# A second buffer for turned keys, and a planner that counts what transfers bring or free as coming later

## The chip, the cores and the metric

The kernel runs on one core of a Trainium2 chip. The metric is device time in microseconds (us). The engines are PE (TensorE, matrix products), DVE (VectorE), ACT (ScalarE), POOL (GpSimd) and SP (SyncE, which here issues every DMA of the kernel body). Each engine works through a list of instructions in a fixed order and waits on semaphores for what the others bring.

## The reference

Block-sparse attention over 4 batches, 8 heads, 768 tokens and 64 features, whose result goes through a feed-forward net with a rational activation:

```python
mask = np.abs(blk_i - blk_j) <= 1            # blocks of 32 tokens, 24 of them
mask = mask | (blk_i == 0) | (blk_j == 0) | (blk_i == n_blocks - 1) | (blk_j == n_blocks - 1)
for qb in range(n_blocks):
    for kb in sampled_blocks[qb]:            # 3 sampled blocks
        mask[qb * 32:(qb + 1) * 32, kb * 32:(kb + 1) * 32] = True
scores = np.where(mask, q @ k.T / sqrt(64), -1e9)
x = softmax(scores) @ v                      # then 3072 tokens of 512 features
h = x @ w_in                                 # w_in 512 x 2048
P = a[0] + a[1] * h + a[2] * h**2 + a[3] * h**3
Q = 1.0 + abs(b[0]) * abs(h) + abs(b[1]) * h**2
out = (P / (Q + 1e-6)) @ w_out               # w_out 2048 x 512
```

## The kernel before

**The work.** The feed-forward net is cut into 12 chunks of 256 tokens, each of 8 units of 256 hidden features, 96 units in all (`unit(c, u)`). PE multiplies a unit into the hidden layer (L1147 to L1149, three products because numbers are kept as a high and a low f16 part), ACT and DVE form the rational function (`sq`, `ab`, `tt`, `rr`, `gh`, `gl`), and PE multiplies it out into `acc` (L1203 to L1205). Attention feeds it: for each block of 32 queries PE makes scores `sp` (L909), DVE the maxima (L919), ACT the exponentials (L937), PE turns them (`pt`, L978), ACT copies them (`pT`, L151), and PE multiplies by the gathered values `vg` (`av`, L1035). Keys come in per block from a scratch array `ks` in DRAM into one of four buffers (`kall` in three parts, and `xkg`), values from `v` into one of three buffers `vg`. Both are loaded by SP: one key or value block is a group of four to six DMAs, three of them at sampled rows (L881, L1005).

**Keys of a batch.** `prep(b)` reads the keys of batch b twice: once for their largest magnitude (ACT, `scrap<-ld`, L398) and once to split them into f16 parts `hl`, which PE turns (`sp<-ident,hl`, L684) into one of two PSUM buffers `sp`. ACT copies these into `kt` (four copies of 0.7 us to a `kt`, L151), and SP stores `kt` into `ks` (L698). A batch has three `kt`. Before the change there is one `kt` buffer, so the copies for the next `kt` wait until the store has read the last one. The same six load buffers `ld` also carry the values, whose largest magnitudes are found by `scrap<-ld` too, and for batches 2 and 3 the queries. For batch 0 the turned keys stay in SBUF.

**The planner.** The order on each engine is not written out. Every step is an `Op` with an engine, a price in ns, a due time and the buffers that it takes and uses; `issue` picks, again and again, the step that could start first by its own clock, and appends it to its engine. A buffer ring (`Ring`) knows when each buffer is free again. A transfer is priced with 475 to 860 ns on SP per DMA, and by its bytes after that. A step that depends on another gets an earliest start `at`, and a later `sure` by which it is ranked; a step of PE that waits for another engine is ranked 1000 ns later. During the first 80 us of its clock it puts dummy products (L163) where it sees PE idle. When the weights are decoded, `switch` closes the pool `early` and opens `ext` with four more `ld` and one more key buffer.

**The start.** Until the first chunk is ready (unit 0), SP loads keys, queries and values of batch 0 and the first pieces of `w_in` (`wl`, L439); POOL, ACT and DVE decode these from 64-bit numbers and split them (`wi`, L155, L512).

Of the kernel before, what the change touches and what calls it, by code (L numbers as in the profile page):

```python
# [13 lines left out]
F16 = mybir.dt.float16  # L14
# [9 lines left out]
def kernel(  # L24
# [28 lines left out]
    B, H, S, D = q.shape  # L53
    DM, DFF = out.shape[1], w_out.shape[0]
    P = 128
    BLK = 32
# [18 lines left out]
    p1 = ctx.enter_context(tc.tile_pool(name="p1", bufs=1))  # L75
    p2 = ctx.enter_context(tc.tile_pool(name="p2", bufs=2))
    p3 = ctx.enter_context(tc.tile_pool(name="p3", bufs=3))
# [18 lines left out]
    VE, SC, PO, TE, SY = "DVE", "Activation", "Pool", "PE", "SP"  # L96
# [68 lines left out]
    def issue(ahead):  # L165
        def work_of(t, price, share):
            for x in (int(t / 3413), int(t / 3413) + 1):
                busy[x] = busy.get(x, 0.0) + share * max(0.0, min(t + price, (x + 1) * 3413) - max(t, x * 3413))

        def tick(t):  # L170
            nonlocal window, warm
            while window < int(t / 3413):
                share = busy.pop(window, 0.0) / 3413
                warm, window = share > (0.45 if warm else 0.85), window + 1

        todo = {e: [] for e in (VE, SC, PO, TE, SY, None)}
        now = dict.fromkeys(todo, 500.0)
        held = 0.0, 0.0
        clock, dma, lanes, quarters = -1.0, 0.0, [0.0] * 8, False
        busy, window, warm = {}, 0, False  # L180
        for n, o in enumerate(plan):
            o.n, o.wait = n, len(o.after) + (o.behind is not None)
            for a in o.after:
                a.next.append(o)
            if o.behind:
                o.behind.next.append(o)
            if not o.wait:
                for e in o.engs:
                    todo[e].append(o)
        left = len(plan)  # L190
        fsh = 0.8
        other = {VE: 500, SC: 534.0, PO: 243.0}
        unit_of = {VE: nc.vector, SC: nc.scalar, PO: nc.gpsimd}
        slack, fend, f00, fgap = 21.0, 80000, 3000, 0
        while left:
            best = None
            for e, l in todo.items():
                for o in l:
                    if o.prio > clock + ahead or not all(s.ring.free for s in o.takes):
                        continue  # L200
                    t = max([now[e], o.at[e]] + [s.ring.free[0][0] for s in o.takes])
                    if e == SY:
                        t = max(t, lanes[0])
                    if e == VE and held[0] <= t < held[1] and o.run.__name__ not in READS_PSUM:
                        t += HELD * (held[1] - t)
                    sure, same = max(t, o.sure[e]), e != TE or o.quarters == quarters
                    key = (max(sure - slack, now[e]) + (0 if e == o.engs[0] else other[e]) + (0 if same else 0), o.prio - (0 if e != TE or not same else 1.0), o.n)
                    if best is None or key < best[0]:
                        best = key, t, o, e
            if best is None:  # L210
                lim = [o for l in todo.values() for o in l]
                raise AssertionError([(o.eng, o.prio, o.run.__qualname__, [len(s.ring.free) for s in o.takes]) for o in lim][:40] + [clock])
            _, t, o, o.eng = best
            e = o.eng
            for x in o.engs:
                todo[x].remove(o)
            for s in o.takes:
                s.buf = s.ring.free.pop(0)[1]
            price = o.alt[e] if o.alt else o.price() if callable(o.price) else o.price
            o.start = t  # L220
            if isinstance(price, list):
                for ns, size in price:
                    t = max(t, lanes.pop(0) if e == SY else t) + ns
                    dma = max(dma, t + 650) + size / 225.0
                    if e == SY:
                        lanes.append(dma + 900)
                end = dma + 900
            elif e == TE:
                f0 = max(now[e], f00)
                while f0 < fend:  # L230
                    tick(f0)
                    f = 213 if warm else 427
                    if f0 + f + fgap > t:
                        break
                    fill()
                    work_of(f0, f, 1.0)
                    f0 += f
                tick(t)
                if now[e] < fend:
                    w = window  # L240
                    x0 = w * 3413
                    for _ in range(2):
                        if not warm or t - x0 < 700 or busy.get(w, 0.0) >= fsh * (t - x0):
                            break
                        fill()
                        work_of(t, 213, 1.0)
                        t += 213
                if not warm:
                    price *= 2 if price > 1100 or price < 500 else 1.8
                if o.quarters != quarters:  # L250
                    t += 93
                    quarters = o.quarters
                work_of(t, price, o.work)
                end = t = t + price
            else:
                end = t = t + price
            now[e] = t
            if e == PO:
                held = o.start, end
            o.end = end  # L260
            o.run(unit_of[e]) if o.alt else o.run()
            if o.unit is not None:
                clock = max(clock, o.unit)
            for s in o.uses:
                s.left -= 1
                s.end = max(s.end, end + (0 if isinstance(price, list) else 200))
                if not s.left:
                    s.ring.free.append((s.end, s.buf))
                    s.ring.free.sort(key=lambda f: f[0])
            for x in o.next:  # L270
                if x.behind is not o:
                    for y in x.engs:
                        lat = MARGIN if isinstance(price, list) else OWN.get(e, 0) if y == e else LAT.get((e, y), 160) + MARGIN
                        x.at[y] = max(x.at[y], end + lat)
                        x.sure[y] = max(x.sure[y], end + lat + (1000 if y == TE and e != TE else 0.0))
                x.wait -= 1
                if not x.wait:
                    for y in x.engs:
                        todo[y].append(x)
            left -= 1  # L280
# [3 lines left out]
    r_gh, r_gl = Ring([None] * 2), Ring([None] * 2)  # L284
    r_ph, r_sp, r_pt, r_acc = Ring([None] * 2), Ring([None] * 2), Ring([None]), Ring([None])
    r_pr, r_st, r_pT, r_av = Ring([None] * 4), Ring([None] * 6), Ring([None] * 2), Ring([None] * 4)
    r_ld, r_hl, r_kt = Ring([p3] * 3), Ring([None] * 2), Ring([None])
    r_ldq, r_hlq, r_qa, r_fc, r_ks = Ring([None]), Ring([None]), Ring([None] * 2), Ring([None] * 2), Ring([None] * 2)
    r_cq, r_scq, r_xn, r_sm = Ring([None] * 4), Ring([None] * 3), Ring([None]), Ring([None] * 2)
    r_wl, r_dw, r_kx, r_sums = Ring([None] * 2), Ring([None] * 3), Ring(range(2)), Ring([None] * 2)  # L290
# [232 lines left out]
    kgs = [kall[:, i * NS:(i + 1) * NS] for i in range(NB // NS)]  # L523
# [113 lines left out]
    s_kt, kts, ext = {}, {}, []  # L637

    def rest(b, w, j, d, o_scale, sc, prio, before):
        first = b == 0  # L640
        t, g = units[j]
# [44 lines left out]
        def evac(e):  # L686
            def run(eng):
                if g == 0 and e == 0:
                    kts[b, t] = kgs[t] if first else p1.tile([P, KB, H, BLK], F16, name="kt")
                dst = kts[b, t][:, :, g * HU:(g + 1) * HU].rearrange("p b h (r s) -> p s h b r", s=2)[:, e]  # L690
                src = d["pt"][:, e].rearrange("p h (b r) -> p h b r", b=KB)
                times(eng, dst, src, 1.0)
            return run
# [7 lines left out]
        sk = s_kall[t] if first else s_kt[b]  # L701
# [612 lines left out]
    for b in range(B):  # L1314
        if b:
            prep(b, when(b))
        for t in range(NT):
            x0 = min(x for x, p in enumerate(parts) if p[0] == b and p[1] // TB == t)
            before = prep_q(b, t, -78.95 if b == t == 0 else part_prio(x0) - (3.23 if x0 >= need[0] else 12.17), before)
            for j in range(t * TB, (t + 1) * TB):  # L1320
                x = next(x for x, p in enumerate(parts) if p[:2] == (b, j))
                attention(b, j, part_prio(x))

    for c, u in order:
        b = c // NCH
# [6 lines left out]
    def switch():  # L1332
        early_cm.__exit__(None, None, None)
        ext.append(ctx.enter_context(tc.tile_pool(name="ext", bufs=1)))
        t = max(o.end for o in decoded + last_near)
        r_ld.free += [(t, ext[0])] * 4
        for j in range(1):
            kgs.append(ext[0].tile([P, NS, H, BLK], F16, name=f"xkg{j}"))
            r_kg.free.append((t, len(kgs) - 1))

    Op(None, 0, switch, decoded + last_near, -1)
    ctx.enter_context(tc.manual_schedule(engines={getattr(mybir.EngineType, n) for n in (TE, SC, VE, PO, SY)}))
    issue(8)
# [29 lines left out]
```

## Time and profile before

| | us |
|---|---|
| median of 3 runs (lowest, highest) | 880.39 (877.9, 882.73) |
| the profiled execution | 884.24 |
| its span on the core | 882.5 |
| PE busy in the span | 814.4 (92%) |
| DVE busy | 729.4 (83%) |
| ACT busy | 668.8 (76%) |
| POOL busy | 115.5 (13%) |

The span is what the trace shows; the execution's time is 1.7 us longer. PE's busy time holds the dummy products of the start, 53.8 us in 201 instructions. The engines' busy times overlap, so a share says little by itself: what counts is when PE stands still, and what it waits for.

### The profile page before, as it was taken

What the parts mean: (1) busy time and instruction counts of PE and PEld (TensorE: products, weight loads), DVE (VectorE), ACT (ScalarE), POOL (GpSimd) and SP (SyncE); (2) the same over time, 40 slices, a digit from 0 to 9 for tenths busy, and PEclk for the clock granted to TensorE, in tenths of its full rate; (3) what the DMA queues carried; (4) which work ended last, traced back from release to release, by engine and by line L of the source; (5) the groups of instructions that cost most, each with busy time, mean ns of one, the idle gap of its engine ahead of it and who ended that gap; (6) DMA issues with size and microseconds to landing.
All of it is one profiled execution on the core that took longest, in us unless ns stands there. A gap on an engine that the chain in (4) does not pass through costs nothing.

```text
span 882.5 us, 27191 instructions
## 1 busy us (share of the span) xinstructions
PE 814.4 (92%) x10339; PEld 648.8 (74%) x10339; DVE 729.4 (83%) x1749; ACT 668.8 (76%) x1445; POOL 115.5 (13%) x119
## 2 busy tenths in 40 slices
PE   8979677777999999999998999969999999999997
PEld 4545565565877788878886888847888888888886
DVE  5667987999997889978895888668788887888996
ACT  6878876996776887898776877948867777776563
POOL 2132631706310000110000000000000000000000
PEclk9999898898999999999999999979999999999999
DMA  7898599785865977889757975787757856560000
GB/s 207 198 175 209 152 195 192 200 217 145 224 160 141 262 205 178 207 235 220 188 144 189 251 204 156 183 222 183 204 148 171 201 141 164 148 160 26 1 25 25
DMA packets 240210, 151.17 MB, mean 171 GB/s; under 512 B 16208, under 2 KB 222928, under 8 KB 240080
## 3 DMA queue, kind: packets, MB, share of 16 engines
q1 hardware_dynamic: 240080, 149.43, 68.5%
q8 instruction: 82, 1.34, 0.7%
q14 instruction: 48, 0.39, 0.2%
HBM read 132.07 MB, written 11.01 MB: 162 GB/s over the span
## 4 chain that ended last, share of the span: by engine, by line
PE 52%; DVE 15%; ACT 13%; DMA 10%; SPq 6%; issue 4%; POOL 0%; ACTq 0%; DVEq 0%; POOLq 0%
PE acc L1203 7%; PE acc L1205 6%; PE acc L1204 6%; PE ph L1147 6%; PE ph L1149 6%; PE ph L1148 6%; PE av L1035 4%; PE pt L978 4%; PE sp L909 3%; DMA vg<-in_v_dram 3%; ACT pr L937 3%; DVE pr L919 2%; PE acc L163 2%; ACT scrap L398 2%; ACT kt L151 2%
## 5 line engine op out<-in xcount | busy, mean ns | idle before, releaser
L1147 PE MATMUL ph<-xh,wi 128*128 128x256 f16 x768 | 213.1, 277 | 7.5 <-DVE tt L1164 7.5
L1148 PE MATMUL ph<-xl,wi 128*128 128x256 f16 x768 | 212.3, 276 | 0.0
L1149 PE MATMUL ph<-xh,wi 128*128 128x256 f16 x768 | 212.1, 276 | 0.0
L1203 PE MATMUL acc<-wo_h,gh 128*128 128x512 f32 x376 | 161.2, 429 | 2.2 <-DVE ld L1263 2.2
L1205 PE MATMUL acc<-wo_h,gl 128*128 128x512 f32 x376 | 150.4, 400 | 0.0
L1204 PE MATMUL acc<-wo_l,gh 128*128 128x512 f32 x376 | 150.3, 400 | 0.0
L1171 DVE SCALAR_TENSOR_TENSOR ab<-sq,absb,ab 128x512 f32<-128x512 f32 x96 | 73.2, 763 | 48.3 <-ACT ab L1168 47.8
L1154 ACT ACTIVATE sq<-ph,fc 128x512 f32<-128x512 f32 x96 | 65.5, 682 | 61.4 <-PE ph L1149 61.3
L937 ACT ACTIVATE pr<-pr,st,cqb 128x256 f32<-128x256 f32 x112 | 66.2, 595 | 41.8 <-DVE st L948 41.8
L1147 PEld LDWEIGHTS <-wi 128*128 128x128 f16 x768 | 76.6, 100 | 24.5 <-issue 13.2
L919 DVE CUSTOM_DVE_ANT_1 pr<-sp,bias 128x256 f32<-128x256 f32 x224 | 84.1, 417 | 10.6 <-PE sp L909 10.6
L1148 PEld LDWEIGHTS <-wi 128*128 128x128 f16 x768 | 76.3, 99 | 15.7 <-issue 6.9
L978 PE MATMUL pt<-ident,pr 128*128 128x128 f32 x448 | 76.0, 292 | 11.6 <-ACT pT L151 7.4
L1203 PEld LDWEIGHTS acc<-wo_h,gh 128*128 128x128 f32 x376 | 72.6, 193 | 18.5 <-issue 2.6
L1182 DVE SCALAR_TENSOR_TENSOR gh<-tt,par,rr 128x512 fp32r<-128x512 f32 x96 | 72.5, 755 | 16.0 <-PE acc L1204 14.2
L1205 PEld LDWEIGHTS acc<-wo_h,gl 128*128 128x128 f32 x376 | 71.8, 191 | 17.4
L1149 PEld LDWEIGHTS <-wi 128*128 128x128 f16 x768 | 76.3, 99 | 9.8
L978 PEld LDWEIGHTS pt<-ident,pr 128*128 128x128 f32 x448 | 66.0, 206 | 22.4 <-ACT pT L151 11.9
L1204 PEld LDWEIGHTS acc<-wo_l,gh 128*128 128x128 f32 x376 | 72.3, 192 | 12.0
L1035 PE MATMUL av<-vg,pT 128*32 128x64 f32 x3584 | 71.4, 224 | 8.0 <-DMA vg<-in_v_dram 5.9
L1035 PEld LDWEIGHTS av<-vg,pT 128*32 128x32 f32 x3584 | 56.5, 111 | 29.7 <-issue 19.2
L1188 DVE SCALAR_TENSOR_TENSOR tt<-tt,par,ab 128x512 f32<-128x512 f32 x96 | 74.8, 779 | 0.9
(164 smaller groups left out, 1670.4 us busy)
## 6 DMA issues: line engine op xcount, KB each, us to landing
vg<-in_v_dram SPq DMA_DIRECT2D x312, 64.0 KB, 3.5
vg<-in_v_dram SPq DMA_DIRECT2D x88, 192.0 KB, 4.4
vg<-in_v_dram SPq DMA_DIRECT2D x24, 512.0 KB, 5.0
kall<-ks SPq DMA_DIRECT2D x52, 192.0 KB, 4.0
kall<-ks SPq DMA_DIRECT2D x156, 64.0 KB, 2.6
ld<-in_k_dram SPq DMA_DIRECT2D x36, 256.0 KB, 4.3
wl<-in_moe_w_in_dram SPq DMA_DIRECT2D x32, 256.0 KB, 4.7
wl<-in_moe_w_out_dram SPq DMA_DIRECT2D x16, 512.0 KB, 4.8
```

What stands on the lines that cost most here:

```text
L919: nc.vector.tensor_tensor_reduce(out=prs[x][:, g].rearrange("p (s r) -> p s r", r=BLK), in0=h["sp"][:, g].rearrange("p (s r) -> p s r", r= ...
L937: nc.scalar.activation(out=prs[x][:, g], in_=prs[x][:, g], func=AF.Exp, scale=Q["first"]["c"], bias=st[:, 6 + g:7 + g], accum_out=total if ...
L978: nc.tensor.transpose(pp[:, jj * P:(jj + 1) * P], cols, ident)
L1035: nc.tensor.matmul(av[rows, g], pT[:, 2 * g + kt, rows] if plain else pT[:, 2 * g + kt, pa_, rows], vf[:, g * HG + h4, kt * D:(kt + 1) * D ...
L1147: nc.tensor.matmul(o, wh, xh[:, :, cc], start=(cc == 0), stop=False)
L1148: nc.tensor.matmul(o, wh, xl[:, :, cc], start=False, stop=False)
L1149: nc.tensor.matmul(o, wl, xh[:, :, cc], start=False, stop=(cc == NCC - 1))
L1171: nc.vector.scalar_tensor_tensor(out=d["ab"], in0=d["sq"], scalar=absb[:, 1:2], in1=d["ab"], op0=ALU.mult, op1=ALU.add)
L1188: nc.vector.scalar_tensor_tensor(out=d["tt"], in0=d["tt"], scalar=par[:, 0:1], in1=d["ab"], op0=ALU.add, op1=ALU.subtract)
L1203: nc.tensor.matmul(acc[:, t], ghs, wo_h[:, f], start=(new and e == 0), stop=False)
L1204: nc.tensor.matmul(acc[:, t], ghs, wo_l[:, f], start=False, stop=False)
L1205: nc.tensor.matmul(acc[:, t], gls, wo_h[:, f], start=False, stop=(last and e == 1))
```

## The change

Four edits. In `issue`, a buffer that a transfer has used counts as free 2000 ns after the transfer's planned end instead of at it, and a step that depends on a step of SP is ranked 2000 ns later. `kt` takes its buffer from a pool that the ring names, and `switch` adds a second one from `ext`, so that from then on (batches 2 and 3) two `kt` are in use.

```diff
             for s in o.uses:
                 s.left -= 1
-                s.end = max(s.end, end + (0 if isinstance(price, list) else 200))
+                s.end = max(s.end, end + (2000 if isinstance(price, list) else 200))
...
-                        x.sure[y] = max(x.sure[y], end + lat + (1000 if y == TE and e != TE else 0.0))
+                        x.sure[y] = max(x.sure[y], end + lat + (1000 if y == TE and e != TE else 0.0) + (2000 if e == SY else 0.0))
...
-    r_ld, r_hl, r_kt = Ring([p3] * 3), Ring([None] * 2), Ring([None])
+    r_ld, r_hl, r_kt = Ring([p3] * 3), Ring([None] * 2), Ring([p1])
...
-                    kts[b, t] = kgs[t] if first else p1.tile([P, KB, H, BLK], F16, name="kt")
+                    kts[b, t] = kgs[t] if first else sk.buf.tile([P, KB, H, BLK], F16, name="kt")
...
         r_ld.free += [(t, ext[0])] * 4
+        r_kt.free += [(t, ext[0])]
```

The two numbers of the planner change the order on every engine from the first microseconds up to about unit 64; behind that, PE's order is the same as before. The work is the same but for two more dummy products (203 for 201) and for steps that may run on either of two engines: POOL gets three fewer conversions, DVE two fewer, ACT five more.

Three places follow. The first is ACT in batch 3, where the keys are copied into `kt` (the numbers tell buffers apart: `ld_10194` is a part of the values, `kt_10354` the second of the three). Before:

```order
L1158 ACTIVATE tt_10257<-ph_10127,par_100,fc_8026 128x512
L151 ACTIVATE pT_10275<-pt_10251 128x512
L1178 ACTIVATE rr_10247<-rr_10247 128x512
L398 ACTIVATE scrap_103,mx_9961<-ld_10194 128x512
L1175 ACTIVATE rr_10318<-ab_10243 128x512
L1178 ACTIVATE rr_10318<-rr_10318 128x512
L151 ACTIVATE kt_10354<-sp_10202 128x4x8x16
L151 ACTIVATE kt_10354<-sp_10261 128x4x8x16
L151 ACTIVATE kt_10354<-sp_10202 128x4x8x16
L151 ACTIVATE kt_10354<-sp_10261 128x4x8x16
```

The same place of ACT now (`kt_10254` is the second `kt`):

```order
L151 ACTIVATE kt_10169<-sp_10184 128x4x8x16
L937 ACTIVATE pr_10049,sm_9925<-pr_10049,st_10048,cqb_6708 128x256 x2
L151 ACTIVATE kt_10254<-sp_10224 128x4x8x16
L1154 ACTIVATE sq_10263<-ph_10151,fc_8043 128x512
L151 ACTIVATE kt_10254<-sp_10224 128x4x8x16
L1168 ACTIVATE ab_10268<-ph_10151,fc_8043 128x512
L1175 ACTIVATE rr_10288<-ab_10108 128x512
L151 ACTIVATE pT_10307<-pt_10270 128x512
L151 ACTIVATE kt_10254<-sp_10279 128x4x8x16
L1178 ACTIVATE rr_10288<-rr_10288 128x512
L151 ACTIVATE kt_10254<-sp_10279 128x4x8x16
```

The second `kt` now begins right behind the first, each `sp` buffer is emptied in turn, and the maximum of a part of the values that stood ahead of the copies has moved behind all twelve of them.

The second place is SP where it asks for the queries of batch 3 (the larger rows around them are one key block ahead and one value block behind). Before:

```order
L881 DMA kall<-ks 128x256
L767 DMA qc<-qa 64x1024
L768 DMA qc<-qa 64x1024
L729 DMA ldq<-in_q_dram 64x4x128 x2
L596 DMA ld<-in_q_dram 128x512 x4
L999 DMA vg_109<-in_v_dram 48x8x128
```

Now, with two value blocks still to come that stood ahead of the query loads before:

```order
L881 DMA kall<-ks 128x256
L596 DMA ld<-in_q_dram 128x512 x3
L999 DMA vg_110<-in_v_dram 48x8x128
L1005 ISA
L1005 DMA vg_110<-in_v_dram 16x8x128
```

The query loads have moved ahead of two value blocks, of an exchange of query halves (L767, L768) and of another load.

The third place is SP in the start, between the first four DMAs of `w_in` (two pieces) and the fourth piece. Before:

```order
L439 DMA wl<-in_moe_w_in_dram 64x1024 x4
...
L768 DMA qc<-qa 64x1024
L596 DMA ld<-in_k_dram 128x512 x3
L439 DMA wl<-in_moe_w_in_dram 64x1024 x2
L999 DMA vg_109<-in_v_dram 48x8x128
...
L439 DMA wl<-in_moe_w_in_dram 64x1024 x2
L999 DMA vg_110<-in_v_dram 48x8x128
```

Now:

```order
L439 DMA wl<-in_moe_w_in_dram 64x1024 x4
L596 DMA ld<-in_k_dram 128x512 x3
...
L439 DMA wl<-in_moe_w_in_dram 64x1024 x2
...
L999 DMA vg_109<-in_v_dram 48x8x128
...
L999 DMA vg_110<-in_v_dram 48x8x128
...
L999 DMA vg_111<-in_v_dram 48x8x128
...
L439 DMA wl<-in_moe_w_in_dram 64x1024 x4
```

The fourth piece stood behind one value block and now stands behind three; the fifth comes with it.

## Rows read from the trace of the kernel before

**Rows 1.** The page: PE's busy share in 40 slices of the span, in tenths.

```profile
PE   8979677777999999999998999969999999999997
```

**Rows 2.** Busy time by stages: length, engines, PE's clock, DMA share, GB/s.

```profile
core 0: us, PE busy (x) PEld busy (x) DVE busy (x) ACT busy (x) POOL busy (x), PEclk, DMA share, GB/s
0.00:72.50 72.50, 62.76 (x790) 34.08 (x791) 44.91 (x155) 53.25 (x138) 19.81 (x29) 0.95 0.87 192
72.50:187.20 114.70, 86.80 (x1326) 66.10 (x1325) 101.91 (x251) 95.18 (x223) 47.74 (x43) 0.90 0.84 193
187.20:257.10 69.90, 61.75 (x783) 48.83 (x781) 69.10 (x168) 53.36 (x113) 28.75 (x24) 0.95 0.69 181
257.10:840.00 582.90, 565.05 (x7221) 469.08 (x7221) 480.00 (x1130) 446.47 (x941) 19.24 (x23) 0.99 0.69 174
```

**Rows 3.** PE's waits: who waited for whom, us in total, times, longest.

```profile
PE sp L684 <- ACT kt L151: 12.9, 3, 7.7
...
PE av L1035 <- DMA vg<-in_v_dram: 5.9, 4, 3.2
PE pt L978 <- ACT pr L937: 4.1, 1, 4.1
```

**Rows 4.** The chain of work that ended last, 563 to 587 us: start, length.

```profile
563.90 0.46 PE sp L684 x8
...
574.33 4.18 DMA ld<-in_v_dram
...
578.53 0.72 ACT scrap L398 x2
...
579.43 3.86 DMA ks<-kt
...
583.32 1.90 ACT kt L151 x3
...
585.26 1.01 PE sp L684 x8
```

**Rows 5.** Busy time around that wait, columns as in rows 2.

```profile
580.00:585.00 5.00, 0.00 (x0) 0.00 (x0) 2.80 (x4) 2.12 (x4) 0.26 (x1) 0.56 0.85 242
585.00:590.00 5.00, 4.74 (x31) 3.15 (x31) 1.53 (x3) 3.17 (x7) 0.69 (x1) 0.50 1.08 238
590.00:595.00 5.00, 5.00 (x40) 4.26 (x39) 4.91 (x14) 2.67 (x7) 0.00 (x0) 0.91 0.92 268
```

**Rows 6.** The tile kt: its copies, waits, and its stores' time to landing.

```profile
L151 ACT ACTIVATE kt<-sp x36: 711/735/787, 154.6 to 597.0; 128x512 f16<-128x512 f16 x36
...
  DMA ks<-kt: 3.2, 2
...
DMA to landing us min/median/max: 3.7/4.5/5.2
```

**Rows 7.** SP at 472 us and before 576 us, instructions in order of time: start, length.

```profile
472.01 2.02 SPq L596 DMA_DIRECT2D ld<-in_q_dram  x4
...
572.81 1.42 SPq L881 DMA_DIRECT2D xkg<-ks  x3
574.33 1.66 SPq L596 DMA_DIRECT2D ld<-in_v_dram  x1
```

**Rows 8.** ACT's wait for queries of batch 3, and busy time after it.

```profile
ACT scrap L398 <- DMA ld<-in_q_dram: 8.4, 1, 8.4
...
478.00:480.00 2.00, 1.96 (x9) 1.38 (x10) 0.25 (x1) 2.00 (x5) 0.00 (x0) 0.56 1.25 184
480.00:485.00 5.00, 5.00 (x31) 3.98 (x30) 4.61 (x9) 5.00 (x13) 0.00 (x0) 0.84 0.90 192
```

**Rows 9.** SP in the start, columns as in rows 7.

```profile
44.29 0.54 SPq L999 DMA_DIRECT2D vg<-in_v_dram  x1
...
50.55 0.38 SPq L999 DMA_DIRECT2D vg<-in_v_dram  x1
```

**Rows 10.** SP's longest wait between 420 and 580 us.

```profile
SPq L876 <- PE av L1035: 1.6, 1, 1.6
```

## The prediction

> **What bounds the kernel now.** I read first the page's slices [rows 1]: after a start with gaps PE is at 9 tenths nearly everywhere from the eleventh slice on, but for an 8 at the twenty-second (463 to 485 us) and a 6 at the twenty-seventh (573 to 596). The table of stages gives the sizes [rows 2]. Up to unit 0 (72.5 us) nothing but dummy products keeps PE busy, and the weights have to come in. From 72.5 to 187.2 us (unit 8) PE lacks 27.9 us while DVE is busy 101.91 of 114.70: DVE, which decodes weights, is the limit. From 187.2 to 257.1 DVE has 69.10 of 69.90, so it is DVE again. From 257.1 to 840 PE has 565.05 of 582.90 at a clock of 0.99: PE is the limit, it lacks 17.9 us, and a wait of PE there moves the end by its length. So I looked for PE's longest waits [rows 3]: `sp` for ACT's copies of turned keys, 12.9 us in 3 waits with a longest of 7.7; the values `vg`, 5.9 in 4; and once 4.1 for the exponentials.
>
> The chain around 580 us shows what the 7.7 are made of [rows 4]. A load of values is issued at 574.33 and has landed at 578.51; behind it ACT finds a maximum, then waits until the store `ks<-kt`, 3.86 us, has ended at 583.3, then copies keys, and PE goes on at 585.26. The clock charges for this once more [rows 5]: in 580 to 585 PE does nothing, and in 585 to 590 its granted clock is 0.50, that is 1.2 in place of 2.4 GHz. Busy time at half clock is worth half: 4.74 × 0.50 = 2.4 us lost, then 5.00 × 0.09 = 0.45, together **2.8**. The Trainium skill ("TensorE: Matmul & The Clock Gate", section Terms) says the same in its formula for the penalty, throttled time times one less the ratio of pulses passed; the trace agrees with it here: eight products of L684 take 1.01 us in the chain's last row at this clock, and took 0.46 in its first [rows 4].
>
> **The change part by part.**
>
> *The second `kt`.* All copies to `kt` are 36 of about 0.735 us, and ACT waits for stores twice, 3.2 us in all [rows 6]. The longer of these, nearly all, is the one in the chain. With a second buffer ACT needn't wait for the store between the first and the second `kt` of batch 3. By itself this is worth at most the 3.86 us of the store in the chain, since the load of values ahead of it in ACT's order still lands at 578.5. The third `kt` now waits for the first store; four copies (2.9 us) lie between and a store takes 4.5 from issue, so without anything between them 1.5 us of wait would be left; the rows of the order show other work of ACT between the copies, which covers it. I take 0.
>
> *The maximum of values behind the copies.* The rank given to what depends on SP moves that step behind all twelve copies. Its load stood behind three key DMAs on SP [rows 7], and ACT stood for it with all its queue: the exponentials, the copies, half of the rational function. Where it now stands, the load has several copies' time (twelve × 0.735 = 8.8 us) more to land, against 4.18 from issue to landing. So the whole PE wait goes, 7.7, and the half clock behind it, 2.8: **−10.5**.
>
> *The queries of batch 3.* ACT waits 8.4 us for them at 467.5 to 475.9 [rows 8]; they are issued at 472.01 [rows 7]. PE waits only the last 4.1 of it [rows 3], so an ACT wait of up to 8.4 − 4.1 = 4.3 is free there. The clock then stands at 0.56 and 0.84: 1.96 × 0.44 + 5.00 × 0.16 = 1.7 lost [rows 8]. On SP the loads have moved ahead of two value blocks, and two of these take 6.3 us of SP in the start (44.29 to 50.55 in [rows 9]), more than the 4.1 that are needed; they have also moved ahead of three other groups. ACT's own step may come earlier too; the 4.3 that are free stand against that. Taken as gone: −4.1 − 1.7 = **−5.8**.
>
> *What is given back.* SP has no slack to do all this: between 420 and 580 us its longest wait is 1.6 us [rows 10], so each load that is moved ahead makes another one later. The two value blocks behind the queries are those, and laid against before's times I find one more such place near 276 us and one near 452 us, with values about 3 us later against PE. The longest wait of PE for values is 3.2 [rows 3]. I price two such waits, 2 × 3.2 = **+6.4**; the bounds are 0 (three buffers hide it) and four of them, 12.8.
>
> *The ring's 2000 ns.* A buffer that PE reads last is freed by PE, later than its load's end plus 2 us; so this bears on `kt` and the query halves that transfers read, and on little else. It moves the order and costs nothing by itself. Two more dummy products run while PE is waiting for unit 0: 0.
>
> *The start.* The fourth piece of `w_in` stands behind two more value blocks, 6.3 us later [rows 9] at worst. Unit 0 needs it. Against that, batch 1's keys are loaded and copied earlier, and ahead of unit 8 fewer steps stand on DVE, while ahead of unit 0 and 2 a few more do. From unit 8 on DVE is full, so only what is late on DVE there counts. I take 0 between the bounds +6.3 (the delay goes through in full) and −12.8 (all of DVE's idle time in 72.5 to 187.2, 114.70 − 101.91, goes [rows 2]); zero, because DVE's total work is the same and it is busy for 89% of that stretch.
>
> *Sum.* −7.7 − 2.8 − 4.1 − 1.7 + 6.4 = −9.9. The profiled execution would go from 884.2 to 874.3; it lies 3.8 above the median of the runs, so the median goes from 880.4 to **870.5**.
>
> **The rivals.** A time within 0.5% (4.4 us, about what a measurement of this kernel can tell) counts as the same.
>
> *B, SP is what is short, and the waits come back elsewhere.* For it: rows 10, and that the change adds no second queue and takes no DMA away. Then only the store's wait really goes, 3.9, and one late value block takes 3.2: −0.7, **879.7**. Against it: the two gaps come from loads asked for just behind others that were not urgent, so order alone can mend them; and ACT's idle time lets it take loads late where nothing waits.
>
> *E, nothing is given back.* The three buffers of `vg` let a value load come 3 us later without PE seeing it: in the whole run of before values made PE wait only four times [rows 3], and one DMA is short to issue beside its way to landing (1.66 and 4.18 us in rows 7 and 4). Then the sum is −7.7 − 2.8 − 4.1 − 1.7 = −16.3: **864.1**. Against it: a block of keys or values takes four to six DMAs, and SP hardly ever waits. The Trainium skill's rule ("DMA: Bandwidth & Descriptors", section "Issuing engines are not separate DMA queues") speaks for E and against B: the sequencer's time to start a DMA is, it says, usually small relative to the DMA itself. For the one DMA of rows 4 and 7 the trace agrees with it; for the whole block no row here does.
>
> *C, slower: weights late in the start.* SP now puts keys and values ahead of pieces of `w_in`. If the 6.3 us are lost not once, for unit 0, but again for each of the next two groups of pieces, three times in all, that is +18.9: **889.4**. It decides from 14.3 us on (9.9 of gain and 4.4), that is from the third loss. For it: PE and DVE both have gaps in that stretch [rows 2]. Against it: the fifth piece now comes right with the fourth, so the delay doesn't add up, and a late piece eats DVE's idle time first.
>
> *D, the start gains too.* Batch 1's keys, ready sooner, let DVE fill its 12.8 us of idle time: 870.5 − 12.8 = **857.7**. The order of DVE ahead of unit 8 speaks for it; I can't see there what DVE would wait for.
>
> *The change does nothing:* were the first edits without effect on late loads, the stall at 580 would hold and 880 come out; the order shows the copies apart from that load, so I count this under B.
>
> **How the numbers follow.** The forecast's chance is 0.48, B 0.22, C 0.12, E 0.12, D 0.06. Low end: E's 864.1, with a third of D's 12.8: **860**. High end: B's 3.9 gained and the start's 6.3 lost in full: **883**; this leaves out most of C and D, some 0.18. Faster by over 0.5%: 0.44 of the forecast's 0.48 (not where four value blocks are late), 0.04 of B, all of D and E: **0.66**. Same: 0.04, 0.16 of B and 0.01 of C: **0.21**. Slower: 0.02 of B and 0.11 of C: **0.13**.
>
> **What the profile after would show.** If right: no wait of PE for `kt` over 2 us behind 257 us, ACT without a wait for `ks<-kt`, no clock of 0.50 near 580, and none below 0.9 near 480; ACT's wait for the queries of batch 3 below 4.3; PE's waits for `vg` up by some 6 us (by 0 under E); unit 0 at 72 to 79 us and unit 8 near 187. B shows as new waits of PE for `vg`, `kall` or `xkg`, together some 15 us, at other places; C as unit 8 at 200 us or later with DVE waiting for `wl`; D as unit 8 before 180. I would be wrong, too, if a wait of ACT on a load moved to a place where exponentials stand right behind it: PE then waits all but 4.3 us of it.

## The result

The changed kernel has a median of 878.64 us (876.31 to 885.8, 20 runs); the kernel before, run beside it, 883.44 (877.9 to 890.37, 20 runs). The ratio is **0.9948, interval 0.9926 to 0.997**: faster by half a per cent, some 4.6 us. The forecast was 9.9 us, so the direction was right and the size about twice too large. The profiled execution took 879.98 us, its span is 878.2.

PE's slices after, from the page:

```profile
PE   8988597596989999989999999879999999999997
```

The 8 of before at 463 to 485 us [rows 1] is gone. The 6 at 573 to 596 has become an 8 and a 7, at 549 to 593 us, and an 8 is new at 373 to 395. PE's waits from 320 to 650 us in the changed kernel (who waited for whom, us in total, times, longest):

```profile
PE pt L978 <- ACT pT L151: 5.3, 4, 2.4
PE sp L684 <- ACT kt L151: 4.6, 2, 4.4
PE sp L909 <- ACT kt L151: 1.2, 1, 1.2
PE sp L909 <- DVE sc L354: 1.0, 1, 1.0
```

Before, the same stretch held one wait of 7.7 and one of 4.1 [rows 3]. Now there are more and smaller ones, and one of 4.4 for `kt`, in batch 2, where there was none. Its chain (start, length):

```profile
369.31 0.42 SPq L596
369.83 3.64 DMA ld<-in_k_dram
373.49 0.19 ACT scrap L398
373.67 0.61 ACT hl L151
374.28 0.62 ACT kt L151
...
376.02 0.63 ACT kt L151
376.69 1.01 PE sp L684 x8
```

This is the picture of [rows 4] again, one batch earlier: a load comes from SP behind a key block, ACT stands for it, and the copies to `kt` stand behind that step. ACT's own wait there was for values (the first row). The chain puts ACT's next step (`hl`) down to a load of keys that landed at 373.47, but that load is the batch's sixth and the step splits the third: in x4 below it runs at 369.62, before that load is asked for (372.50). The next late load that something stood for came 3.0 us behind the values, on POOL: queries (the second row).

```profile
372.95 0.63 ACT L398 ACTIVATE scrap<-ld 128x512 f16<-128x512 f32 x1 [4.03 <-DMA ld<-in_v_dram]
...
375.98 0.69 POOL L155 TENSOR_SCALAR hlq<-ldq,scqb 128x512 f16<-128x512 f32 x1 [9.02 <-DMA ldq<-in_q_dram]
...
583.57 0.75 ACT L151 ACTIVATE kt<-sp 128x512 f16<-128x512 f16 x1 [2.82 <-DMA ks<-kt]
```

The last row, in batch 3, is the third `kt`, which waits for the store of the first. The clock charges for the wait at 372 as it did at 580 [rows 5] (columns as in rows 2):

```profile
370.00:375.00 5.00, 2.32 (x23) 1.64 (x21) 0.98 (x4) 2.05 (x5) 0.00 (x0) 0.99 0.78 215
375.00:380.00 5.00, 3.31 (x20) 2.68 (x21) 4.03 (x7) 5.00 (x11) 2.75 (x3) 0.50 1.07 181
380.00:385.00 5.00, 5.00 (x33) 4.21 (x32) 2.97 (x5) 3.65 (x6) 0.69 (x1) 0.83 0.89 230
```

3.31 × 0.50 + 5.00 × 0.17 = 2.5 us. Near 480 and 580 the clock now stays at 1.00.

To see where the time went I take each kernel's profiled execution apart at four units, by the start of the unit's first product (L1147) on PE. Behind unit 24 the counts of PE's products between these units are the same in all kernels. Ahead of it the kernels with the later rank run 31 more products before unit 0 and 29 fewer from there to unit 24; 21 and 19 of these are dummies. All lengths are in us, and the third column is the ratio of the runs' times with its interval.

| kernel | span | ratio | to unit 0 | 0–24 | 24–40 | 40–64 | 64–end |
|---|---|---|---|---|---|---|---|
| before | 882.5 | | 72.5 | 253.2 | 128.1 | 200.8 | 227.9 |
| changed | 878.2 | 0.9948 (0.9926–0.997) | 71.9 | 251.9 | 131.1 | 195.4 | 227.9 |
| x1 buffer, old order | 877.1 | 0.9955 (0.9928–0.9981) | 70.5 | 254.4 | 129.8 | 194.5 | 227.9 |
| x2 numbers, one buffer | 883.6 | 1.0018 (0.9994–1.0042) | 73.9 | 251.4 | 132.3 | 197.9 | 228.1 |
| x3 buffer, old numbers | 874.3 | 0.9971 (0.9945–0.9997) | 68.2 | 253.5 | 127.9 | 192.1 | 232.6 |
| x4 changed, one maximum moved | 874.8 | 0.9939 (0.991–0.9967) | 73.0 | 251.2 | 131.9 | 190.6 | 228.0 |
| x5 changed, loads by POOL | 864.7 | 0.9861 (0.9834–0.9888) | 72.1 | 250.8 | 127.7 | 185.9 | 228.3 |
| x6 before, loads by POOL | 870.2 | 0.9892 (0.9863–0.9921) | 73.6 | 254.4 | 125.9 | 188.0 | 228.2 |
| x7 buffer, loads by POOL | 868.3 | 0.983 (0.98–0.9861) | 74.2 | 253.9 | 127.8 | 184.0 | 228.3 |
| x8 buffer and maximum | 883.3 | 1.0016 (0.9991–1.004) | 69.5 | 253.7 | 128.8 | 198.5 | 232.8 |
| x9 numbers early, loads by POOL | 868.1 | 0.9895 (0.9863–0.9926) | 71.2 | 254.6 | 126.9 | 187.2 | 228.2 |
| x10 batch 1 too | 879.4 | 0.9971 (0.9946–0.9996) | 77.3 | 254.2 | 132.5 | 187.1 | 228.3 |
| x11 rank and buffer | 879.9 | 0.999 (0.997–1.001) | 71.6 | 254.6 | 131.1 | 194.7 | 227.9 |
| x12 ring and buffer | 876.0 | 0.9967 (0.9948–0.9986) | 70.4 | 257.3 | 133.6 | 186.7 | 228.0 |

A length of one execution isn't the mean: x3's profiled execution took 876.05 us, its twelve runs have a median of 880.4. So a column tells a difference of 5 us or more, and smaller ones only where several kernels agree; the ratios decide. In the changed kernel 40–64 gained 5.4 us where I expected 16.3 less 6.4, and 24–40 lost 3.0.

### The profile page after: what moved, and what is told of

Read it like the earlier page. It is cut to its first block, busy times and chain, and to the rows that moved or that the text cites. A ratio compares the mean times of both kernels' runs of the same rounds, so it can differ in the third digit from the quotient of the medians.

```text
span 878.2 us, 27204 instructions
## 1 busy us (share of the span) xinstructions
PE 810.4 (92%) x10341; PEld 644.9 (73%) x10341; DVE 731.8 (83%) x1748; ACT 670.8 (76%) x1450; POOL 113.5 (13%) x115
## 2 busy tenths in 40 slices
DMA packets 240210, 151.17 MB, mean 172 GB/s; under 512 B 16208, under 2 KB 222928, under 8 KB 240080
## 3 DMA queue, kind: packets, MB, share of 16 engines
q1 hardware_dynamic: 240080, 149.43, 67.2%
## 4 chain that ended last, share of the span: by engine, by line
PE 55%; DVE 16%; DMA 9%; ACT 8%; SPq 5%; issue 4%; POOL 2%; ACTq 0%; POOLq 0%; DVEq 0%
PE acc L1203 7%; PE acc L1205 7%; PE acc L1204 7%; PE ph L1147 7%; PE ph L1149 6%; PE ph L1148 6%; PE av L1035 4%; PE pt L978 4%; PE sp L909 3%; DMA ld<-in_k_dram 2%; ACT pr L937 2%; DVE pr L919 2%; DMA wl<-in_moe_w_in_dram 1%; DMA vg<-in_v_dram 1%; DVE tt L1188 1%
## 5 line engine op out<-in xcount | busy, mean ns | idle before, releaser
L1147 PE MATMUL ph<-xh,wi 128*128 128x256 f16 x768 | 213.3, 278 | 1.6 <-DVE tt L1164 1.6
L1203 PE MATMUL acc<-wo_h,gh 128*128 128x512 f32 x376 | 158.8, 422 | 0.3 <-DVE ld L1263 0.2
L1147 PEld LDWEIGHTS <-wi 128*128 128x128 f16 x768 | 76.4, 99 | 22.1 <-issue 12.7
L1203 PEld LDWEIGHTS acc<-wo_h,gh 128*128 128x128 f32 x376 | 71.5, 190 | 16.3 <-issue 2.3
L937 ACT ACTIVATE pr<-pr,st,cq 128x256 f32<-128x256 f32 x112 | 66.1, 593 | 22.5 <-DVE st L948 22.3
L1204 PEld LDWEIGHTS acc<-wo_l,gh 128*128 128x128 f32 x376 | 71.2, 189 | 13.6 <-POOL wo_l L465 0.9
L1164 DVE SCALAR_TENSOR_TENSOR tt<-ph,fc,tt 128x512 f32<-128x512 f32 x96 | 71.7, 747 | 4.8 <-DVE tt L1161 0.5
L1158 ACT ACTIVATE tt<-ph,par,fc 128x512 f32<-128x512 f32 x96 | 75.1, 782 | 0.0
```

The lines of the kernel that those rows point to most:

```text
L937: nc.scalar.activation(out=prs[x][:, g], in_=prs[x][:, g], func=AF.Exp, scale=Q["first"]["c"], bias=st[:, 6 + g:7 + g], accum_out=total if ...
L1147: nc.tensor.matmul(o, wh, xh[:, :, cc], start=(cc == 0), stop=False)
L1158: nc.scalar.activation(out=d["tt"], in_=d["ph"], func=AF.Identity, scale=d["cst"][:, 3:4], bias=par[:, 2:3])
L1203: nc.tensor.matmul(acc[:, t], ghs, wo_h[:, f], start=(new and e == 0), stop=False)
L1204: nc.tensor.matmul(acc[:, t], ghs, wo_l[:, f], start=False, stop=False)
```

## The experiments

**Theory A** (the forecast): the two gaps are single steps that stand in the wrong place; the buffer is worth up to 3.9 us, the planner's numbers the rest. **Theory B** (the rival of the prediction): SP's one queue brings batch 2's and 3's loads late, so a step moved out of a late load's way uncovers the next late load.

**x1, the buffer alone, every order as before.**

```diff
-kts[b, t] = kgs[t] if first else p1.tile([P, KB, H, BLK], F16, name="kt")
+kts[b, t] = kgs[t] if first else (ext[0] if ext and t == 1 else p1).tile([P, KB, H, BLK], F16, name="kt")
```

> The kernel before with every instruction in its old order; only the second kt of batches 2 and 3 goes to a second buffer, without the planner knowing. If the stall at 577 to 585 us is a late load of values and behind it a store, PE's wait of 7.7 there shrinks by about the store's share, to some 3.8 to 4.3, ACT's wait for the store is gone, and the span falls by 4 to 5 us. If SP's queue is what holds batch 3 up (rival B), the wait moves to the third kt or to another load and the span stays within 2 us.

Measured 0.9955, some 4 us and nearly the whole gain of the change: the expectation's first branch, not B's. PE's waits from 320 to 650 us are now these:

```profile
PE sp L909 <- ACT kt L151: 2.7, 1, 2.7
PE sp L684 <- DVE st L919: 2.7, 1, 2.7
PE pt L978 <- ACT pr L937: 2.2, 1, 2.2
...
PE sp L684 <- ACT kt L151: 0.5, 1, 0.5
```

The 7.7 are down to 0.5 beside a new 2.7 for DVE. ACT no longer waits for `ks<-kt` at all. Behind the second row stands POOL, which waits 5.66 us at 581.75 for queries (`ldq`), and DVE for POOL: the next late load, and a first sign of what B says.

**x2, the numbers alone**, with the one buffer: only the two lines of `issue` from the diff.

> The changed kernel's two planner numbers with the one kt buffer of before. If the second buffer is needed for the gain, ACT waits for the store between the first and the second kt in batch 2 and 3 and PE waits 5 us or more for kt in one of them: 880 to 888 us. If the numbers alone carry the gain, it is as fast as the changed kernel, about 878.6.

Measured 1.0018: the numbers by themselves gain nothing. In batch 3 PE's wait of 7.7 for `kt` is down to 2.7, with one buffer. But PE waits 5.4 for `kt` in batch 2, where before it had no such wait, and 3.6 for the exponentials at 478, nearly as before.

**x3, the buffer alone, known to the planner**: only the lines of the diff on `kt`.

> The second kt buffer, known to the planner, with the old planner numbers. Up to unit 32 as before. If the two gaps of before are separate things, PE's wait for the queries of batch 3 (4.1) stays or returns and the stall for kt falls under 4: 874 to 880 us. If only the planner numbers bring order into the loads, the stall for kt stays above 6 and the time stays at 880 to 884.

Measured 0.9971 (880.4 us), at the edge of the first branch. The wait for the queries stays (2.6 us at 470), and PE's wait for `kt` near 580 is gone. The 40–64 part is short, but a wait of 2.4 comes up at 662 us, in a part that no other run but x8 slows down.

**x4, in the changed kernel the maximum ahead of batch 2's copies moved behind them** (one instruction of ACT; DVE's order changes behind it, PE's and SP's don't).

```diff
-return Op(SC, 613, most, [before[w]], prio, uses=[slot])
+return Op(SC, 613, most, [before[w]] + (k_evac[b, NCH - 1][-1:] if (b, w, j) == (2, 1, 2) else []), prio, uses=[slot])
```

> The changed kernel with one instruction of ACT moved: the maximum of the third part of batch 2's values now stands behind the copies to kt; PE's and SP's orders are the same. If the wait of 4.4 us at 372 and the slow clock behind it (about 5 per cent of 65 us) are an added loss of the changed kernel, they go and the span falls by 5 to 7 us, to 871 to 873. If PE's time in batch 2 and 3 is set by when SP's loads come (rival B), the wait comes back within the next units and the span falls by under 2.

Measured 0.9939, against 0.9948 for the changed kernel. ACT now reaches the first copy to `kt` at 370.25 and not at 374.19, and the third group of key products no longer waits. But the fourth now does, for 5.0 us; it starts at 380.16, and started at 380.91 in the changed kernel. First a row of POOL, then one of DVE, then the chain behind them:

```profile
377.54 0.69 POOL L155 TENSOR_SCALAR hlq<-ldq,scqb 128x512 f16<-128x512 f32 x1 [10.09 <-DMA ldq<-in_q_dram]
...
378.93 1.17 DVE L392 SCALAR_TENSOR_TENSOR hl<-ld,sc,hl 128x512 f16<-128x512 f32 x1 [6.15 <-POOL hl L155]
...
378.93 1.18 DVE hl L392
380.11 0.05 issue
380.16 1.03 PE sp L684 x8
```

ACT stood for values that SP brought late; with that out of the way, POOL stands for queries that SP asks for two DMAs later, and the split of keys that PE needs is behind them in POOL's order. 24–40 stays at 131.9, and the gain over the changed kernel is some 0.8 us. This is B's branch.

**x5, x6, x7: the loads by POOL.** POOL is busy for 19.24 of 582.90 us behind unit 16 [rows 2], so it can ask for loads. The keys, values and queries that `prep` and `prep_q` load for batches 2 and 3 (L546, L596, L729) are issued by it, 76 DMAs by the trace of x7, where the expectation has 54. What is read, its bytes and the orders of PE, DVE and ACT stay. One of the three changed lines, cut short:

```diff
-nc.sync.dma_start(out=d["ld"], ...
+(nc.gpsimd if b >= QB else nc.sync).dma_start(out=d["ld"], ...
```

In the changed kernel (x5):

> The changed kernel; the loads of keys, values and queries that prep makes for batches 2 and 3 (54 DMAs) are issued by POOL, in the places the planner gave them, and SP has only the rest. PE's, DVE's and ACT's orders are the same. If SP's one queue is what brings these loads late (rival B), PE's waits between 320 and 650 us (some 10 us idle and a slow clock at 372) shrink by half or more and the span falls by 5 to 10 us, to 868 to 873. If the 16 DMA engines or POOL's own order hold them, the waits stay within 2 us of the changed kernel's, or grow where POOL stands for a free buffer.

In the kernel before (x6):

> The kernel before, one kt buffer, same orders on PE, DVE and ACT; the same loads go to POOL. If SP's queue is behind both gaps of before, the 4.1 at 474 goes and the 7.7 at 577 shrinks to about 3 (the store, which then comes earlier too, may hide wholly): 870 to 876 us. If not SP but the way to landing is what is late, both gaps stay within 1 us: 880 to 885.

In x1 (x7):

> The kernel before in its old order with the second kt buffer (as in the run with the buffer alone in the same order) and the loads by POOL. If buffer and queue are separate causes, their gains add: 4 us from the one and 4 to 6 from the other, 868 to 874 us. If they are the same microseconds, it is no faster than the better of the two alone.

Measured 869.64, 872.17 and 868.67 us, beside 882.73 of before: by the ratios (0.9861, 0.9892, 0.983) 12.3, 9.5 and 15.0 us less. All three lie in the range of the branch that blames SP's queue, and the gains of buffer and queue add, 4 and 9.5 us, within what the intervals tell. In x6, with the one buffer, the query wait is gone and the stall of 7.7 is down to what the store costs (PE's waits from 320 to 650 us):

```profile
PE sp L684 <- ACT kt L151: 2.6, 1, 2.6
PE sp L909 <- ACT kt L151: 0.4, 1, 0.4
```

With the buffer as well (x7) PE has no gap left in 454 to 650 us; the row of that window, columns as in rows 2:

```profile
454.00:650.00 196.00, 195.90 (x2621) 164.13 (x2621) 167.89 (x400) 160.91 (x347) 34.78 (x52) 1.00 0.87 206
```

The same window had 183.93 us of PE in the kernel before and 185.78 in the changed one. What moved can be read off SP. The store of batch 3's first `kt`, the second row here, was issued at 579.43 before [rows 4], 10.8 us behind the last copy to that `kt` (568.64); in x7 it is 2.6 us behind it (564.50). x7, start and length:

```profile
565.66 1.36 SPq L881 DMA_DIRECT2D kall<-ks  x3
567.12 0.40 SPq L698 DMA_DIRECT2D ks<-kt  x1
...
574.75 0.41 SPq L698 DMA_DIRECT2D ks<-kt  x1
```

The loads themselves got little or no quicker. Their issue takes POOL 0.55 to 0.58 us at L596 (mean of the three groups), and to landing the page gives for keys, median in us, for x7 and then for the kernel before (whose row has batch 1 too):

```profile
ld<-in_k_dram POOLq DMA_DIRECT2D x24, 256.0 KB, 5.6
```

```profile
ld<-in_k_dram SPq DMA_DIRECT2D x36, 256.0 KB, 4.3
```

Keys and queries take longer on the way (values 3.9 against 4.3), and the kernel is faster: what was late was their turn in SP's queue.

POOL's loads also go through a queue of their own, as the page of x7 shows (packets, MB, share of the 16 engines' span):

```profile
q1 hardware_dynamic: 221968, 133.70, 64.6%
q0 software_dynamic: 5120, 15.73, 6.8%
```

Before, q1 had 240,080 packets and 149.43 MB, for 68.5%: the 15.73 MB that it lost are q0's, in 5,120 packets and not 18,112. So x5 to x7 change the queue and the size of the packets along with the engine that issues. Lighter transfers are not the reason: both queues together take 71.4% of a span of 868.3 us, more time than the 68.5% of 882.5. Whether a second queue without a second issuing engine would do as much, no run shows.

**x8, x1 with the maximum of batch 3's third part of values behind the copies** (x4's edit with batch 3 in place of 2, on x1). The planner re-orders what comes behind it.

> The kernel before with the second kt buffer and the maximum of the third part of batch 3's values put behind the copies (what the planner's numbers did in batch 3); orders change only behind that place. By my sum the maximum is worth 6.6 us on top of the buffer's 3.9: 871 to 874 us. If moving one late load only uncovers the next (as in batch 2), it is as the buffer alone, 877 to 880.

Measured 1.0016, outside both ranges: the buffer's gain is gone. PE waits 2.5 and 3.5 us before two groups of L684 at 574 and 582, and 3.3 at 653. Only the first two speak of the maximum. Up to 593 us nothing but it has moved in any engine's order, and they are 6.0 us where x1 has 3.2 for the same groups: x8 is 2.8 us ahead at unit 40, but POOL starts on its keys at 570.44 and on its queries at 582.49, as in x1 (570.48 and 581.75), and stands for both. So the loads set the pace there, and the moved step gains nothing. The third lies where PE's order is new (595 to 621 us) or behind it, as do the 4.9 us that x8 loses from unit 64 on; x3 loses as much there without this edit.

**x9, x10: is there a better mixture?** x9 has the numbers up to unit 20 and the old ones behind, x1's buffer and the loads by POOL; x10 gives POOL the loads of batch 1 too. One line of x9:

```diff
-s.end = max(s.end, end + (2000 if isinstance(price, list) else 200))
+s.end = max(s.end, end + ((2000 if clock < 20 else 0) if isinstance(price, list) else 200))
```

> The changed planner numbers up to unit 20 only, the old ones from there on; second kt buffer outside the planner's knowledge, prep's loads of batches 2 and 3 issued by POOL. The stretch from unit 0 to 24 was 253 to 254 us with the old numbers and 251 to 252 with the new: if that is theirs, this gains some 2 us on the buffer with loads by POOL (868.7), 865 to 868. If the numbers are worth nothing there either, 868 to 870.

> As the run before, and batch 1's loads too are issued by POOL. If SP's queue delays weights in the start, the stretch from unit 0 to 24 shrinks by 2 to 5 us. If POOL, which decodes weights then (its 47 us of 107 busy), is held up by waiting for load buffers, the stretch grows and the time is 870 or more.

x9 comes to 873.58 us (0.9895), outside both ranges: no better than x7, and 0–24 is 254.6, so the shorter stretch of the changed kernel is not simply the numbers'. x10 is 881.01 (0.9971): unit 0 starts at 77.3 us, later than in any other run, PE waits 4.5 at 378, and POOL now stands for load buffers that ACT empties:

```profile
POOL ld L596 <- ACT scrap L398: 36.5, 10, 6.8
```

**x11, x12: each number with the buffer**, loads by SP: the changed kernel without the first or the second changed line of `issue`.

> The changed kernel without the ring's 2000 ns: only the later rank and the second buffer, loads by SP. If the numbers only shuffle which load is late, this lies between the buffer alone (880) and the numbers alone (885), with a stretch from unit 40 to 64 of 192 to 198 us. If the rank is the number that orders the loads well, it is faster than the changed kernel, under 877.

> The changed kernel without the later rank: only the ring's 2000 ns and the second buffer, loads by SP. If the numbers only shuffle, 878 to 885 as in the run before, and the stretch from unit 40 to 64 stays above 190; if the ring's number is the harmful or the useful one, it stands 3 us or more away from the changed kernel.

881.67 (0.999) and 879.97 us (0.9967). Neither beats the buffer alone in the old order, and x11 lies where shuffling was to put it. x12 leaves it open: 40–64 is 186.7, under the 190 that shuffling was to give, but 0–24 and 24–40 are the longest of all, 257.3 and 133.6, and eat it.

## Why the prediction was half right

**The second buffer: right.** "Worth at most the 3.86 us of the store" measured 0.45% in x1, 4.0 us (1.7 to 6.4 by its interval), and in x7 against x6 the 40–64 part is 4.0 shorter. That the third `kt` costs nothing was wrong in the changed kernel: ACT stands 2.82 us for the first store, and a PE wait of 2.4 at 586 stands behind it. SP issues that store 8 us after its last copy (578.36 against 570.7).

**The maximum behind the copies, −6.6 of the −10.5: gone at its place, but not worth its price.** I reasoned that where the step now stands, its load has time, "so the whole PE wait goes". It did go there: no wait for `kt` at 577 to 585, and a clock of 1.00. But in batch 2, and in batch 3 up to 593 us, x4 and x8 move such a step by itself and gain 0.8 us or nothing: the next load in SP's queue is as late, and another engine stands for it. A step moved out of the way is worth at most the distance to the next late load, 3.0 us in batch 2 of the changed kernel (372.95 and 375.98), and PE got some 0.8 of it.

**The queries of batch 3, −5.8: gone in the changed kernel** (the clock near 480 is 1.00), but not by the numbers as such, since x2 has them and PE waits 3.6 there. PE's 4.1 were not "the last 4.1" of ACT's wait, either: they ran from 473.96 to 478.04, and ACT's ended at 475.9.

**What is given back, +6.4: this is the step that failed, in size and in place.** The two gaps forecast as gone, 16.3 us, lie between unit 40 and 64, and that part is only 5.4 us shorter; 24–40 is 3.0 longer. So some 13.9 us came back (16.3 − 5.4 + 3.0, of single executions), more than twice the 6.4 and over the bound of 12.8. I priced it as two waits of 3.2 for values in `vg`, but PE's waits for these fell, from 5.9 [rows 3] to 1.1. It came back as keys, values and queries that `prep` and `prep_q` load: 4.4 and 2.5 of clock in batch 2, and in batch 3 waits of 0.5 to 2.4 us. Of the idle time from unit 40 to 64 (12.1 us before) 10.2 are still there. With these loads off SP's queue the time falls by 7.7 us (x5 against the changed kernel, by the ratios).

**The start, 0: right as a sum, not on the way.** Unit 0 starts at 71.9; the fourth piece of `w_in` came at 50.2 us (53.3 before) and not later, and nothing was lost. Unit 24 comes 1.9 us earlier. But unit 8, forecast near 187, comes at 179.5, which was D's sign (columns as in rows 2):

```profile
71.89:179.49 107.60, 78.56 (x1313) 59.49 (x1311) 97.32 (x235) 90.77 (x215) 46.71 (x41) 0.89 0.80 196
179.49:262.68 83.19, 71.11 (x831) 54.05 (x830) 82.11 (x195) 62.11 (x132) 29.63 (x25) 0.92 0.71 185
```

From unit 0 to 8 the changed kernel is 7.1 us shorter than before [rows 2], and from 8 to 16 it is 13.3 longer, with DVE busy for 82.11 of 83.19; from 16 to 24 7.4 come back. All kernels with either of the numbers show this: 104.7 to 110.5 us from unit 0 to 8 and 83.2 to 88.2 from 8 to 16, where the others have 113.1 to 117.2 and 68.9 to 69.9. So the numbers move DVE's work into the stretch from unit 8 to 16 and take none of it away: D's sign came, its gain didn't. (Nor is it only dummy products that keep PE busy up to unit 0, as the prediction reads rows 2: they are 45.4 of its 62.76 us.)

**Theory B** forecast 879.7 and named its sign, "new waits at other places". The median of 878.64 is near that by luck: the kernel before ran at 883.44 beside it, and not at 880.39, so B's gain of 0.7 stands against 4.6. B's size was off too. But x5 to x7 show its cause: without a byte less to move, a second engine that issues, with its queue, gains 9.5 us where the planner's numbers gain none. B, too, had the place wrong: it named `vg`, `kall` and `xkg`, and the late loads were those of `prep` and `prep_q`. My argument against B, that the gaps come from loads asked for behind others that aren't urgent, so that order alone can mend them, is what x2, x4 and x11 contradict. The rule of the Trainium skill that spoke for E, that starting DMAs on several engines saves only the sequencer's time, which is usually small beside the DMA itself ("DMA: Bandwidth & Descriptors", section "Issuing engines are not separate DMA queues"), holds for a single DMA here (the store of rows 4 takes 0.40 us to issue and 3.86 to land) and misleads for their sum: with 76 of them elsewhere SP issued the store 2.6 us behind its last copy and not 10.8. E itself, nothing given back, is contradicted by the changed kernel, x2 and x4. SP's slack was small, not nil: from 420 to 580 us its waits add up to 17 of 160 us in the kernel before, and to 0.6 in the 14 us from 566 on, ahead of the stall.

What stays open: why single kernels' early stretches differ by 3 to 6 us with the numbers (x11, x12 in 0–24), and how much of the changed kernel's 0.5% is the buffer's and how much chance of the new order; x1's and the changed kernel's intervals overlap almost wholly. Open, too, is how much of x5 to x7 is SP's time to issue and how much the queue behind it.

## What to carry to other kernels

Before a wait for a transfer is costed as gone, look at what stands next in the queue of the engine that issues it: if that queue has next to no idle time there, the gain of a moved step ends at the next late load. Ask what the queue would do with less in it, and try that first: here an idle engine that issued some of the loads brought twice what the change did, and with the buffer three times. And a new order from a planner is a new draw; test the part that doesn't need it (here the buffer, in the old order) by itself. x3 and x8 each lost some 4.8 us behind unit 64 to such a draw.

## What the runs showed that I had not expected

Loads issued by POOL are dearer to issue than by SP (medians of 0.54 to 0.59 us against 0.43 to 0.50 at L596, and 0.76 against 0.43 at L546), and keys are 1.3 us slower to land (5.6 against 4.3), and still x7 is 1.7% faster than before. In x7 PE is busy 195.90 of 196.00 us with DVE at 167.89 and a DMA share of 0.87, higher than the 0.76 of before in the same window: the 16 DMA engines had not been full.
